# A fused attention and MLP kernel: where the seven-product quads stand, and when their operands are made

## The chip, the cores and the metric

The kernel runs on one core of one Trainium2 chip. The core's engines work side by side, each through its own queue of instructions: TensorE (PE, matmuls into PSUM; PEld is its weight load), VectorE (DVE), ScalarE (ACT), GpSimd (POOL), and SyncE (SP), which here only issues DMAs. The metric is the time of one execution on the device, in microseconds; smaller is better.

## The reference

Block-sparse attention over 4 batches, 8 heads, 768 tokens and 64 values per head, and behind it a residual MLP with affine layers, on tokens of 512 values:

```python
scores = scale * np.matmul(q, k.transpose(0, 1, 3, 2))
mask = ...   # diagonal blocks of 32, first and last block, 3 sampled blocks per row
attn = softmax(np.where(mask, scores, -1e9))
x = np.matmul(attn, v)            # laid out as (batch, token, 512)
a1 = alpha1 * x + beta1
tok = np.einsum('ts,bsd->btd', w_tok, a1)
u = x + lam * tok
a2 = alpha2 * u + beta2
ch = np.maximum(a2 @ w_ch1, 0.0) @ w_ch2      # 512 -> 2048 -> 512
out = u + lam * ch
```

## The kernel before

**Attention.** The 32 heads are 16 pairs (`i`, four to a batch). A pair is nine units of scores: `emit_qk` (L600), exponential on ACT (`emit_exp`, L618), the product with the 0/1 mask on VectorE (`emit_keep`, L635, only from pair 5 on; before, the mask lies in the score matmul), the value matmuls (`emit_pv` L647, `emit_pv_keys` L670), and `emit_finish`: a reciprocal (L687) and the normalisation (L688) into the batch's `x_sb`. `emit_a1pp` (L704, L705), mostly on POOL, makes the affine input of the token mixer; `job_tok2` (L844, L856) is the mixer.

**MLP.** For each batch, `job_f1` (L910, ACT L917) makes hidden rows: `hts[(b, c)]` holds 16 rows of 128 for half `c` of the tokens (three tiles of 128 each). The second layer has two forms:

- *direct*, `job_f2` (L930): one token tile times all of `w2b`, 16 matmuls of 512 columns in four quarters (`g`), then one addition into `x_sb` (L939) and a store;
- a *quad* (`job_p`, `mul` L1044): two token tiles together, by the Winograd form of Strassen's scheme. The operands are cut in two along hidden rows and along output columns, and seven products of 8 matmuls with 256 columns take the place of eight. In a quad, "11" and "12" are the two hidden halves of its first tile, "21" and "22" those of its second.

What the products need beside `hts` and `w2b`: sums and differences of hidden rows S1 to S4 (`job_s`, L1018; S3 and S4 overwrite "21" and "12"), and differences of weights T1, T2, T4, T3 (`job_t`, L972), 16 subtractions of two rows each, kept in the attention's freed q and k buffers. After each product `plus` (L1054) adds its bank to `x_sb` on VectorE. Products 1, 6 and 5 add up in one bank, and so do 7 and 4; each addition has to read the bank before the next product of the chain goes on in it.

**Order.** It is written out by hand. Up to pair 4 a table, `PLAN`, gives each job a slot ("tq5", the transposes of pair 5's q, has slot 31.62). Behind that come rows of letters (`W1`, `W2`, `W2L`, `W3`), three rows for a pair. A row is emitted letter by letter into all queues: `q` the scores of the row's three units and their first exponential, `x` another exponential, `k` a mask product, `p` value matmuls, `f` a hidden row, `g` the next step of the second layer, `S` a hidden-row sum, `A` a weight difference, `T` a mixer step, `L` the loads of a later pair, `Y` the copy of its values, `Q` and `K` its transposes by DMA, `d` and `v` transposes of the mixer's result. Batch 1's second layer runs in `W2` (pairs 8 to 11), batch 2's in `W2L` (pairs 12 to 15), batch 3's in `W3` and after. An engine's queue holds its instructions in the order in which the letters emit them.

`STR` lists the batches with quads, `P_ORDER` the order of `g`, `S_ORDER` that of `S`:

```python
STR = (2, 3)
P_ORDER[2] = direct 0, product 2 of quads 1 and 2, direct 3, product 1 of both,
             then products 6, 7, 5, 4, 3 of quad 1 and of quad 2
P_ORDER[3] = three quads
```

A quad `t` before consists of the tiles `t` and `t + 3`, one from each half of the tokens.

Of the kernel before, what the change touches and what calls it, by code (L numbers as in the profile page):

```python
# [52 lines left out]
]  # L53
W2 = [
# [12 lines left out]
]  # L67
W2L = [
# [12 lines left out]
]  # L81
W3 = [
# [4 lines left out]
]  # L87
STR = (2, 3)
HN = NH // 2
HC = DM // 2  # L90
WEAVE = W1 + W2 + W2L + W3
# [96 lines left out]
    "mask2": 30.13,  # L188
    "w2_1": 30.13,
    "w1_1": 30.27,  # L190
    "tq5": 31.62,
    "tok2_0": 31.97,
    "lv5": 32.09,
    "mask13": 32.27,
# [53 lines left out]
def kernel(  # L248
# [16 lines left out]
    nc = tc.nc  # L265
# [194 lines left out]
    def sp_tile():  # L460
        return psum.tile([P, 2, 512], FP, name="sp", tag="sp", bufs=2)
# [6 lines left out]
    def mm_tile(shape=(P, DM), dt=FP):  # L468
        return psum.tile(list(shape), dt, name="mm", tag="mm", bufs=3)
# [103 lines left out]
    x_sbs = {}  # L573
# [237 lines left out]
    hts = {}  # L811
# [177 lines left out]
    def a_of(b, t, name, r=slice(0, HN)):  # L989
        if name in ("X1", "X2"):  # L990
            return xs[(b, t, name)][:, r]
        c, half = {"11": (0, 0), "12": (0, 1), "21": (1, 0), "22": (1, 1)}[name]
        return hts[(b, c)][:, HN * half + r.start : HN * half + r.stop, ts(t, P)]

    SOP = {
        1: ("X1", "21", "22", ALU.add),
# [5 lines left out]
    def job_s(b, t, n, r=slice(0, HN)):  # L1002
        dst, a, c, op = SOP[n]
        rows = range(r.start, r.stop)
        for name in (a, c):
            if name[0] == "X":
                assert all(("S", b, t, int(name[1]), m) in did for m in rows)
            else:
                h, half = divmod(int(name) - 11, 10)
                assert all(("f", b, h, HN * half + m) in did for m in rows)  # L1010
        if n == 3:
            assert all(("S", b, t, 1, m) in did for m in rows)
        if n == 4:
            assert (b, t, 2) in did
        if dst[0] == "X" and (b, t, dst) not in xs:
            tag, bufs = ("eT", 6) if b == B - 1 else ("xs", 4)
            xs[(b, t, dst)] = ap_.tile([P, HN, P], BF, name="xs", tag=tag, bufs=bufs)
        nc.vector.tensor_tensor(  # L1018
            out=a_of(b, t, dst, r), in0=a_of(b, t, a, r), in1=a_of(b, t, c, r), op=op
        )  # L1020
        did.update(("S", b, t, n, m) for m in rows)
# [12 lines left out]
    def mul(b, t, n, ps, start, cols=slice(0, HC)):  # L1034
        a, m, need = PROD[n]
        assert m in bq or all((m, r) in did for r in range(0, HN, 2))
        if need:
            assert all(("S", b, t, need, r) in did for r in range(HN))
        c, half = {"1": (0, 0), "X": (1, 0)}.get(a[0], (1, 0))
        if need == 0:  # L1040
            h, half = divmod(int(a) - 11, 10)
            assert all(("f", b, h, HN * half + r) in did for r in range(HN))
        for r in range(HN):
            nc.tensor.matmul(  # L1044
                ps,
                a_of(b, t, a)[:, r],
                b_rows(m, r)[:, 0, cols],
                start=(start and r == 0),
                stop=(r == HN - 1),
                skip_group_check=True,  # L1050
            )

    def plus(x, ps):
        nc.vector.tensor_tensor(out=x, in0=x, in1=ps, op=ALU.add)  # L1054

    def twice(ps):
        return ps.unsqueeze(1).broadcast_to([P, 2, HC])

    lo, hi = slice(0, HC), slice(HC, DM)

    def job_p(b, t, n):
        x = x_sbs[b]
        last = (b, t) == (B - 1, NT // 2 - 1)
        bk = banks.setdefault((b, t), {})
        if n in (1, 2, 7):
            bk[n] = sp_tile()[:, 0] if n == 1 else mm_tile()[:]
        if n == 3 and not last and 2 not in bk:
            bk[2] = mm_tile()[:]
        if n == 1:
            mul(b, t, 1, bk[1][:, lo], True)  # L1070
            plus(x[:, t, lo], bk[1][:, lo])
        elif n == 2:
            mul(b, t, 2, bk[2][:, lo], True)
            if last or b < B - 1:
                plus(x[:, t, lo], bk.pop(2)[:, lo])
            if last:
                emit_store(b, t, lo)
        elif n == 6:
            mul(b, t, 6, bk[1][:, lo], False)
            plus(x[:, t + 3, lo], bk[1][:, lo])  # L1080
        elif n == 7:
            mul(b, t, 7, bk[7][:, lo], True)
            plus(x[:, t + 3, hi], bk[7][:, lo])
        elif n == 5:
            mul(b, t, 5, bk[1][:, lo], False)
            plus(x[:, t : t + 4 : 3, hi], twice(bk[1][:, lo]))
        elif n == 4:
            mul(b, t, 4, bk[7][:, lo], False)
            plus(x[:, t + 3, lo], bk[7][:, lo])
            emit_store(b, t + 3, slice(0, DM))  # L1090
        elif last:
            for h in range(2):
                sl = slice(HC + h * P, HC + h * P + P)
                ps = (mm_tile(), op_tile([P, DM]))[h]
                mul(b, t, 3, ps[:, sl], True, ts(h, P))
                plus(x[:, t, sl], ps[:, sl])
                emit_store(b, t, sl, (nc.sync, nc.scalar)[h])
        else:
            sl = hi if b < B - 1 else slice(0, DM)
            mul(b, t, 3, bk[2][:, hi], b < B - 1)  # L1100
            plus(x[:, t, sl], bk[2][:, sl])
            emit_store(b, t, slice(0, DM))
        did.add((b, t, n))

    NPAIR = B * NP
# [34 lines left out]
    def start_mlp(b):  # L1140
        ns = [n // 2 + HN * (n % 2) for n in range(NH)] if b == B - 1 else range(NH)
        todo["f"] += [lambda c=c, n=n: job_f1(b, c, n) for c in range(2) for n in ns]
        if b not in STR:
            todo["g"] += [
# [6 lines left out]
        ]  # L1151
        todo["S"] += [lambda t=t, n=n, r=r: job_s(b, t, n, r) for t, n, r in S_ORDER[b]]

    REST = (6, 7, 5, 4, 3)
    P_ORDER = {
        2: [(0, g, "g") for g in range(4)]
        + [(t, 2) for t in (1, 2)]
        + [(3, g, "g") for g in range(4)]
        + [(t, 1) for t in (1, 2)]
        + [(t, n) for t in (1, 2) for n in REST],  # L1160
        3: [(t, n) for t in range(2) for n in (1, 2)]
        + [(t, n) for t in range(2) for n in REST]
        + [(2, n) for n in (1, 2) + REST],
    }
    ALL, R1, R2 = slice(0, HN), slice(0, HN // 2), slice(HN // 2, HN)
    S_ORDER = {
        2: [(t, n, ALL) for t in (1, 2) for n in (1, 2, 3, 4)],
        3: [(t, n, R1) for n in (1, 2, 3) for t in range(3)]
        + [(t, n, r) for t in range(3) for n, r in ((1, R2), (2, R2), (3, R2), (4, ALL))],
    }  # L1170

    def start_pair(i):
# [222 lines left out]
```

## Time and profile before

| | |
|---|---|
| median of 3 runs | 300.59 us (300.05 to 300.66) |
| the profiled execution | 300.64 us |
| its span, first to last instruction | 298.6 us |
| mean granted TensorE clock | 1.000 |
| busy: PE, DVE, ACT, POOL | 292.3, 219.5, 218.6, 109.7 us |
| hidden rows, L910: 512 matmuls | 91.6 us |
| direct form, L930: 224 matmuls of 512 columns | 54.7 us |
| quad products, L1044: 272 matmuls of 256 columns, 16 of 128 | 38.1 us, by groups |

A timeline row has the start, the time from the first start to the last end of a merged group, engine and line, what is written from what, the shape and the count, and in brackets idle time of the engine just before, with what ended it. A row of groups has the busy time, the mean of one in ns, and the idle time ahead. A matmul's own row is longer than the distance to the next one, because they are pipelined; distances are what adds up on TensorE.

### The profile page before, as it was taken

The numbers are of one execution on the slowest core, as the hardware profiler recorded it, in microseconds if no ns is written. First come the engines' busy times: TensorE is split into PE (matmuls) and PEld (weight loads), VectorE is DVE, ScalarE is ACT, GpSimd is POOL, SyncE is SP. The second block draws the span as 40 slices with busy tenths as digits, with TensorE's granted clock in tenths as the row PEclk, the third lists the DMA queues.
The fourth block names the chain that finished last, engine by engine and source line by source line (L and its number), as shares of the span: only waits on it lengthen the run. The fifth ranks groups of instructions, "written<-read, shape, count | busy, mean of one in ns | idle before, by whom it ended". The sixth has DMA issues, their size and how long they took to land.

```text
span 298.6 us, 7517 instructions
## 1 busy us (share of the span) xinstructions
PE 292.3 (98%) x3113; PEld 194.5 (65%) x3113; DVE 219.5 (74%) x434; ACT 218.6 (73%) x324; POOL 109.7 (37%) x149
## 2 busy tenths in 40 slices
PE   7999999999999999999999999999999999999995
PEld 3688888665567565565576465565566589666884
DVE  4988999995678797978778777892756889204674
ACT  4999999998799963999779581999869734677100
POOL 8997887632443710355323340344320300000000
PEclk9999999999999999999999999999999999999999
DMA  6999999971392992729844777727321112300032
GB/s 178 201 193 168 192 156 204 190 121 26 94 151 50 120 201 75 121 61 134 119 85 76 121 119 143 114 72 89 50 61 30 25 37 57 113 0 2 0 140 74
DMA packets 57273, 31.08 MB, mean 104 GB/s; under 512 B 37204, under 2 KB 54016, under 8 KB 57240
## 3 DMA queue, kind: packets, MB, share of 16 engines
q0 software_dynamic: 16752, 14.22, 33.2%
q1 hardware_dynamic: 40020, 15.92, 27.9%
q8 instruction: 24, 0.39, 0.6%
q10 hardware_dynamic: 468, 0.47, 0.5%
q14 instruction: 9, 0.07, 0.1%
HBM read 29.75 MB, written 6.29 MB: 121 GB/s over the span
## 4 chain that ended last, share of the span: by engine, by line
PE 83%; DVE 6%; DMA 6%; ACT 3%; POOL 1%; issue 1%; ACTq 0%; SPq 0%; POOLq 0%
PE mm L910 27%; PE mm L930 15%; PE sp L600 8%; PE mm L844 8%; PE op L670 7%; PE mm L1044 5%; PE sp L1044 4%; PE mm L600 3%; DMA qpad<-in_q_dram 3%; ACT eT L618 2%; PE op L647 2%; DVE eT L635 2%; PE mm L820 1%; DMA uraw<-ubf 1%; DMA ms<-ms_c 1%
## 5 line engine op out<-in xcount | busy, mean ns | idle before, releaser
L618 ACT ACTIVATE eT<-sp,expb 128x1024 f16<-128x1024 f32 x111 | 118.4, 1120 | 2.2 <-PE sp L600 1.6
L910 PE MATMUL mm<-uT,w1b 128*128 128x384 bf16 x512 | 91.6, 326 | 0.1
L635 DVE TENSOR_TENSOR eT<-eT,mask 128x1024 f16<-128x1024 f16 x99 | 80.3, 840 | 13.9 <-ACT eT L618 13.7
L917 ACT ACTIVATE hts<-mm 128x384 bf16<-128x384 f32 x128 | 60.9, 500 | 16.5 <-PE mm L910 15.9
L704 POOL TENSOR_TENSOR a1pp<-x_sb,vbc 128x384 bf16<-128x384 f32 x25 | 28.5, 1140 | 119.3 <-DVE x_sb L688 85.3
L910 PEld LDWEIGHTS <-w1b 128*128 128x128 bf16 x512 | 48.1, 98 | 32.0 <-issue 2.4
L618 ACT ACTIVATE eT<-mm,expb 128x512 f16<-128x512 f32 x66 | 41.7, 685 | 26.5 <-PE mm L600 26.2
L930 PE MATMUL mm<-w2b,hts 128*128 128x512 bf16 x224 | 54.7, 379 | 0.0
L670 PEld LDWEIGHTS <-eT 128*128 128x128 f16 x792 | 29.8, 98 | 8.7 <-issue 1.7
L930 PEld LDWEIGHTS <-hts 128*128 128x128 bf16 x224 | 19.8, 98 | 22.3 <-issue 3.9
L670 PE MATMUL op<-vext,eT 128*128 128x65 f16 x792 | 32.1, 194 | 0.1
L600 PE MATMUL sp<-qTs,kTs 88*128 88x512 bf16 (+1 forms) x120 | 26.9, 326 | 1.4 <-ACT eT L618 0.7
L705 POOL TENSOR_TENSOR a1pp<-a1pp,vbc 128x384 bf16<-128x384 bf16 x25 | 26.7, 1069 | 2.0
L844 PE MATMUL mm<-a1pp,wtokT 128*128 128x256 bf16 x216 | 25.9, 273 | 0.1
L844 PEld LDWEIGHTS <-wtokT 128*128 128x128 bf16 x216 | 20.6, 98 | 5.6 <-issue 1.8
L1044 PEld LDWEIGHTS <-hts 128*128 128x128 bf16 x208 | 19.6, 98 | 3.0 <-issue 0.3
L600 PE MATMUL sp<-qhT,khT 64*128 64x256 bf16 (+1 forms) x176 | 19.8, 322 | 0.0
L856 DVE TENSOR_TENSOR x_sb<-x_sb,mm 128x512 f32<-128x512 f32 x18 | 12.3, 685 | 9.9 <-PE mm L844 9.8
L600 PEld LDWEIGHTS <-khT 64*128 64x128 bf16 x264 | 10.6, 94 | 12.7 <-issue 9.2
L647 PEld LDWEIGHTS <-eT 128*128 128x128 f16 x360 | 14.9, 98 | 3.8 <-issue 0.3
L1018 DVE TENSOR_TENSOR xs<-hts 128x512 bf16<-128x512 bf16 (+1 forms) x8 | 3.7, 487 | 17.8 <-ACT hts L917 17.8
L688 DVE TENSOR_TENSOR x_sb<-op,rcp 128x384 f32<-128x384 f32 x28 | 15.6, 557 | 1.0
(117 smaller groups left out, 322.3 us busy)
## 6 DMA issues: line engine op xcount, KB each, us to landing
out_dram<-x_sb SPq DMA_DIRECT2D x23, 256.0 KB
qpad<-in_q_dram POOLq DMA_DIRECT2D x15, 192.0 KB, 4.6
kr<-in_k_dram POOLq DMA_DIRECT2D x15, 192.0 KB, 5.6
vr<-in_v_dram POOLq DMA_DIRECT2D x15, 192.0 KB, 6.2
w1b<-in_moe_w_ch_dram POOLq DMA_DIRECT2D x4, 512.0 KB, 9.3
w2b<-in_moe_w_ch_dram POOLq DMA_DIRECT2D x4, 512.0 KB, 8.4
hts<-in_moe_w_tok_dram POOLq DMA_DIRECT2D x2, 576.0 KB, 9.2
x_sb<-in_k_dram ACTq DMA_DIRECT2D x2, 192.0 KB
```

The source lines that it names most:

```text
L600: nc.tensor.matmul(sp[jj][:, dst], lhsT, rhs, start=True, stop=True, skip_group_check=True,)
L618: nc.scalar.activation(dst, at, AF.Exp, bias=expb[:], scale=SCALE)
L635: nc.vector.tensor_mul(out=e, in0=e, in1=keep)
L647: nc.tensor.matmul(op[0][:, o, :], ets[u][:, jj, h * QB + n * P : h * QB + n * P + P], vexts[i % NVB][:, w, 2 * jp + jj, :], start=op[1] == 0,
L670: nc.tensor.matmul(op[0][:, o, :], ets[u][:, jj, h * QB + n * P : h * QB + n * P + P], vexts[i % NVB][:, w, 2 * jp + jj, :], start=op[1] == 0,
L704: eng.tensor_tensor(out=dst, in0=x_sbs[b][:, :, cols], in1=bc[0], op=ALU.mult)
L705: eng.tensor_tensor(out=dst, in0=dst, in1=bc[1], op=ALU.add)
L844: nc.tensor.matmul(ps[:, o], wtokT[:, os_, ts(2 * n + o, P)], a1pps[i][:, os_, :], start=(os_ == 0 and o == 0), stop=(os_ == NT - 1 and o ...
L910: nc.tensor.matmul(ps[:, 0:QC], w1b[:, dk, ts(n, P)], uTs[b][:, dk, ts(c, QC)], start=(dk == 0), stop=(dk == 3),)
L917: nc.scalar.activation(hts[(b, c)][:, n, :], ps[:, 0:QC], AF.Relu)
L930: nc.tensor.matmul(ps[:], ht[:, nk, ts(o % 3, P)], w2b[:, nk, :], start=(nk == 0), stop=(nk == NH - 1),)
L1044: nc.tensor.matmul(ps, a_of(b, t, a)[:, r], b_rows(m, r)[:, 0, cols], start=(start and r == 0), stop=(r == HN - 1), skip_group_check=True,)
```

## The change

A quad now takes two tiles of the same half of the tokens in batches 1 and 2, so that it needs one `hts` half only; `t` is a pair of tile numbers. Batch 1, all direct before, gets the quad (0, 1); batch 2's two are (0, 1) and (3, 4), in place of (1, 4) and (2, 5); batch 3's three stay (0, 3), (1, 4), (2, 5). Product 1 of batch 1's quad and of batch 2's first takes a bank of the three shared `mm` banks, not one of scores (`sp`). The products of a quad follow each other without another quad's in between. The 16 letters `A` move from `W2` rows 5, 6 and 9 to `W1` rows 3, 4, 5 and 8 and `W2` rows 0, 2 and 5; the letters `S` go to rows 7 and 9 of `W2` and `W2L` and, for batch 2's second quad, stay in `W3`; one `g` of `W2` falls away, two `f` leave `W2L` rows 7 and 8, one comes back in its row 11, one in `W3`. The slot of "tq5" is 32.6.

```diff
-    "q K x g p k 0 k 1 x Q p L Y f f g 2 g k",
-    "q g g x x 0 1 f k 2 k f p k p",
-    "q 0 s 1 s k x x p T f 2 k f k p",
+    "q A A K x g p k 0 k 1 x Q p L Y f f g 2 g k",
+    "q A A A g g x x 0 1 f k 2 k f p k p",
+    "q A A A 0 s 1 s k x x p T f 2 k f k p",
...
-    "q 0 x p x g k k 1 d g k g 2",
+    "q A A 0 x p x g k k 1 d g k g 2",
 ]
 W2 = [
-    "q 0 p p g k x L x p f k 1 K 2 k",
+    "q A A 0 p p g k x L x p f k 1 K 2 k",
...
-    "q g 0 k g d 1 2 p x k g x k",
+    "q A A A g 0 k g d 1 2 p x k g x k",
...
-    "q k 0 f x f p s f f x 1 L p k 2 f f f k Y A A A A A f",
-    "q f L f 0 f k A A A A A A A A 1 f Y x f p g x f p f g k k 2",
-    "q x k x k Q 0 g 1 s f f g p 2 p f f k p",
+    "q k 0 f x f p s f f x 1 L p k 2 f f f k Y A f",
+    "q f L f 0 f k 1 f Y x f p g x f p f g k k 2",
+    "q S S x k x k Q 0 g 1 s f f g p 2 p f f k p",
     "q T 0 k f 1 x k f T x f 2 p k K p",
-    "q A A A x 0 x T k 1 k f 2 k f Q f d p L",
+    "q S S x 0 x T k 1 k f 2 k f Q f d p L",
     "q x 0 x K k g d k s f g f 1 k p p g 2",
-    "q Y g x x k g k f 0 1 k 2 p g v g v",
+    "q Y g x x k g k f 0 1 k 2 p g v v",
 ]
 W2L = [
...
-    "q x k x k Q 0 g 1 s f f g p 2 p f f k p f",
-    "q T 0 k f 1 x k f T x f 2 p k K p f",
-    "q x 0 x T k 1 k f 2 k f Q f d p L",
-    "q x 0 x K k g d k s f g f 1 k p p S S g 2",
-    "q p Y x x k g k S 0 1 k 2 g v g v g",
+    "q S S x k x k Q 0 g 1 s f f g p 2 p f f k p",
+    "q T 0 k f 1 x k f T x f 2 p k K p",
+    "q S S x 0 x T k 1 k f 2 k f Q f d p L",
+    "q x 0 x K k g d k s f g f 1 k p p g 2",
+    "q p Y x x k g k f 0 1 k 2 g v g v g",
 ]
 W3 = [
-    "a p p p g s g g T S T S T S S S d g g U g v g g g g g f f f f",
+    "a p p p f g s g T S T S T S d g g U g v S g g g g g g f f f f",
...
-STR = (2, 3)
+STR = (1, 2, 3)
...
-    "tq5": 31.62,
+    "tq5": 32.6,
...
-        c, half = {"11": (0, 0), "12": (0, 1), "21": (1, 0), "22": (1, 1)}[name]
-        return hts[(b, c)][:, HN * half + r.start : HN * half + r.stop, ts(t, P)]
+        o, half = t[int(name[0]) - 1], int(name[1]) - 1
+        return hts[(b, o // 3)][:, HN * half + r.start : HN * half + r.stop, ts(o % 3, P)]
...
-        if n in (1, 2, 7):
-            bk[n] = sp_tile()[:, 0] if n == 1 else mm_tile()[:]
-        if n == 3 and not last and 2 not in bk:
-            bk[2] = mm_tile()[:]
+        if n == 1 and (tail or (b == B - 2 and o1 == 3)):
+            bk[1] = sp_tile()[:, 0]
+        elif n in (1, 2, 7) or (n == 3 and not tail):
+            bk[n] = mm_tile()[:]
...
+    def direct(*tiles):
+        return [(o, g, "g") for o in tiles for g in range(4)]
+
+    def quad(t, order):
+        return [(t, n) for n in order]
+
     REST = (6, 7, 5, 4, 3)
     P_ORDER = {
-        2: [(0, g, "g") for g in range(4)]
-        + [(t, 2) for t in (1, 2)]
-        + [(3, g, "g") for g in range(4)]
-        + [(t, 1) for t in (1, 2)]
-        + [(t, n) for t in (1, 2) for n in REST],
+        1: quad((0, 1), (2, 1, 6, 5, 7, 4, 3)) + direct(2, 3, 4, 5),
+        2: quad((0, 1), (2, 1, 6, 5, 7, 4, 3))
+        + direct(2, 5)
+        + quad((3, 4), (2, 1) + REST),
...
     S_ORDER = {
-        2: [(t, n, ALL) for t in (1, 2) for n in (1, 2, 3, 4)],
+        1: [((0, 1), n, ALL) for n in (1, 2, 3, 4)],
+        2: [(t, n, ALL) for t in ((0, 1), (3, 4)) for n in (1, 2, 3, 4)],
```

More of the change, by code (lines that the diff above doesn't have):

```diff
@@ L991, in a_of, with a_ready @@
             return xs[(b, t, name)][:, r]
-        c, half = {"11": (0, 0), "12": (0, 1), "21": (1, 0), "22": (1, 1)}[name]
-        return hts[(b, c)][:, HN * half + r.start : HN * half + r.stop, ts(t, P)]
+        o, half = t[int(name[0]) - 1], int(name[1]) - 1
+        return hts[(b, o // 3)][:, HN * half + r.start : HN * half + r.stop, ts(o % 3, P)]
+    def a_ready(b, t, name, rows):
+        if name[0] == "X":
+            return all(("S", b, t, int(name[1]), m) in did for m in rows)
+        o, half = t[int(name[0]) - 1], int(name[1]) - 1
+        return all(("f", b, o // 3, HN * half + m) in did for m in rows)
     SOP = {
@@ L1004, in job_s @@
         rows = range(r.start, r.stop)
[L1005 to L1010, printed above, removed]
+        assert a_ready(b, t, a, rows) and a_ready(b, t, c, rows)
         if n == 3:
@@ L1038, in mul @@
             assert all(("S", b, t, need, r) in did for r in range(HN))
[L1039 to L1042, printed above, removed]
+        assert a_ready(b, t, a, range(HN))
         for r in range(HN):
@@ L1061, in job_p @@
     def job_p(b, t, n):
-        x = x_sbs[b]
-        last = (b, t) == (B - 1, NT // 2 - 1)
+        x, (o1, o2) = x_sbs[b], t
+        tail = b == B - 1
+        last = tail and o2 == NT - 1
         bk = banks.setdefault((b, t), {})
-        if n in (1, 2, 7):
-            bk[n] = sp_tile()[:, 0] if n == 1 else mm_tile()[:]
-        if n == 3 and not last and 2 not in bk:
-            bk[2] = mm_tile()[:]
+        if n == 1 and (tail or (b == B - 2 and o1 == 3)):
+            bk[1] = sp_tile()[:, 0]
+        elif n in (1, 2, 7) or (n == 3 and not tail):
+            bk[n] = mm_tile()[:]
         if n == 1:
             mul(b, t, 1, bk[1][:, lo], True)
-            plus(x[:, t, lo], bk[1][:, lo])
+            plus(x[:, o1, lo], bk[1][:, lo])
         elif n == 2:
             mul(b, t, 2, bk[2][:, lo], True)
-            if last or b < B - 1:
-                plus(x[:, t, lo], bk.pop(2)[:, lo])
+            if last or not tail:
+                plus(x[:, o1, lo], bk[2][:, lo])
             if last:
-                emit_store(b, t, lo)
+                emit_store(b, o1, lo)
         elif n == 6:
             mul(b, t, 6, bk[1][:, lo], False)
-            plus(x[:, t + 3, lo], bk[1][:, lo])
+            plus(x[:, o2, lo], bk[1][:, lo])
         elif n == 7:
             mul(b, t, 7, bk[7][:, lo], True)
-            plus(x[:, t + 3, hi], bk[7][:, lo])
+            plus(x[:, o2, hi], bk[7][:, lo])
         elif n == 5:
             mul(b, t, 5, bk[1][:, lo], False)
-            plus(x[:, t : t + 4 : 3, hi], twice(bk[1][:, lo]))
+            plus(x[:, o1 : o2 + 1 : o2 - o1, hi], twice(bk[1][:, lo]))
         elif n == 4:
             mul(b, t, 4, bk[7][:, lo], False)
-            plus(x[:, t + 3, lo], bk[7][:, lo])
-            emit_store(b, t + 3, slice(0, DM))
+            plus(x[:, o2, lo], bk[7][:, lo])
+            emit_store(b, o2, slice(0, DM))
         elif last:
@@ L1095, in job_p @@
                 mul(b, t, 3, ps[:, sl], True, ts(h, P))
-                plus(x[:, t, sl], ps[:, sl])
-                emit_store(b, t, sl, (nc.sync, nc.scalar)[h])
-        else:
[L1099 to L1102, printed above, removed]
+                plus(x[:, o1, sl], ps[:, sl])
+                emit_store(b, o1, sl, (nc.sync, nc.scalar)[h])
+        else:
+            sl, ps = (slice(0, DM), bk[2]) if tail else (hi, bk[3])
+            mul(b, t, 3, ps[:, hi], not tail)
+            plus(x[:, o1, sl], ps[:, sl])
+            emit_store(b, o1, slice(0, DM))
         did.add((b, t, n))
@@ L1152, in start_mlp @@
         todo["S"] += [lambda t=t, n=n, r=r: job_s(b, t, n, r) for t, n, r in S_ORDER[b]]
+    def direct(*tiles):
+        return [(o, g, "g") for o in tiles for g in range(4)]
+    def quad(t, order):
+        return [(t, n) for n in order]
     REST = (6, 7, 5, 4, 3)
     P_ORDER = {
-        2: [(0, g, "g") for g in range(4)]
-        + [(t, 2) for t in (1, 2)]
-        + [(3, g, "g") for g in range(4)]
-        + [(t, 1) for t in (1, 2)]
-        + [(t, n) for t in (1, 2) for n in REST],
-        3: [(t, n) for t in range(2) for n in (1, 2)]
-        + [(t, n) for t in range(2) for n in REST]
-        + [(2, n) for n in (1, 2) + REST],
+        1: quad((0, 1), (2, 1, 6, 5, 7, 4, 3)) + direct(2, 3, 4, 5),
+        2: quad((0, 1), (2, 1, 6, 5, 7, 4, 3))
+        + direct(2, 5)
+        + quad((3, 4), (2, 1) + REST),
+        3: quad((0, 3), (1, 2))
+        + quad((1, 4), (1, 2))
+        + quad((0, 3), REST)
+        + quad((1, 4), REST)
+        + quad((2, 5), (1, 2) + REST),
     }
     ALL, R1, R2 = slice(0, HN), slice(0, HN // 2), slice(HN // 2, HN)
+    Q3 = [(0, 3), (1, 4), (2, 5)]
     S_ORDER = {
-        2: [(t, n, ALL) for t in (1, 2) for n in (1, 2, 3, 4)],
-        3: [(t, n, R1) for n in (1, 2, 3) for t in range(3)]
-        + [(t, n, r) for t in range(3) for n, r in ((1, R2), (2, R2), (3, R2), (4, ALL))],
+        1: [((0, 1), n, ALL) for n in (1, 2, 3, 4)],
+        2: [(t, n, ALL) for t in ((0, 1), (3, 4)) for n in (1, 2, 3, 4)],
+        3: [(t, n, R1) for n in (1, 2, 3) for t in Q3]
+        + [(t, n, r) for t in Q3 for n, r in ((1, R2), (2, R2), (3, R2), (4, ALL))],
     }
```

## The prediction

> **What bounds the kernel now.** I read the page's busy times and slices first, then the chain of waits, then the timeline engine by engine around the places that the change touches.
>
> ```profile
> span 298.6 us, 7517 instructions
> PE 292.3 (98%) x3113; PEld 194.5 (65%) x3113; DVE 219.5 (74%) x434; ACT 218.6 (73%) x324; POOL 109.7 (37%) x149
> PE   7999999999999999999999999999999999999995
> PE 83%; DVE 6%; DMA 6%; ACT 3%; POOL 1%; issue 1%; ACTq 0%; SPq 0%; POOLq 0%
> ...
> 99.62 2.59 PE mm L930 x12
> 254.04 1.75 PE mm L1044 x16
> ```
>
> TensorE (PE) works in every slice and makes 83% of the chain, so a microsecond taken from it is a microsecond gained, and one in which it waits is lost. VectorE (DVE), at 74%, has room, but its rows follow the program's order: one that waits holds up all behind it. From the last two rows: a 512-column matmul of the direct form takes 2.59/12 = 0.216 us, a 256-column matmul of a quad product 1.75/16 = 0.109 us.
>
> **The arithmetic saved.** Two direct tiles are 2 x 16 x 0.216 = 6.91 us; a quad is 7 x 8 x 0.109 = 6.1 us. Batch 1 gains one quad, batch 2 keeps two: **-0.8 us** on TensorE, certain, as nothing else is removed there.
>
> **Pair 5's q, delayed.** Its six transposes wait for their load; tok2_0's six matmuls, two score matmuls and eight value matmuls now go first.
>
> ```profile
> 39.51 0.41 PE L647 MATMUL op<-vext,eT 128*128 128x65 f16 x8
> 40.17 0.51 PE L550 MATMUL mm<-ident,qpad 128*128 128x128 bf16 x6 [0.24 <-DMA qpad<-in_q_dram]
> 53.28 0.47 DVE L885 TENSOR_SCALAR uT<-mm,ab2T 128x384 bf16<-128x384 bf16 x1
> 53.34 1.47 PE L910 MATMUL mm<-uT,w1b 128*128 128x384 bf16 x8
> ```
>
> Eight value matmuls of 0.03 us from 39.51 leave some 0.4 us idle before 40.17. But VectorE is what comes next: its scaling that ends at 53.75 is awaited by the fourth matmul of the group begun at 53.34, which starts at 53.83. That chain shortens little. I take **-0.2**, bounds -0.4 and 0. The step's three VectorE copies go behind one value copy, with pair 5's first use far later; it issues no DMA.
>
> **The weights' differences, moved.** Sixteen subtractions leave VectorE near 135-140 and 156 us for six groups of 2, 3, 3, 2, 2 and 3 in earlier idle stretches, and one alone.
>
> ```profile
> 139.11 0.76 DVE L972 TENSOR_TENSOR kTs<-w2b,kTs 128x512 bf16<-128x512 bf16 x2
> 76.12 0.69 DVE L939 TENSOR_TENSOR x_sb<-x_sb,mm 128x512 f32<-128x512 f32 x1 [0.86 <-PE mm L930]
> 86.13 0.69 DVE L635 TENSOR_TENSOR eT<-eT,mask 128x1024 f16<-128x1024 f16 x1 [1.16 <-ACT eT L618]
> 118.05 0.69 DVE L635 TENSOR_TENSOR eT<-eT,mask 128x1024 f16<-128x1024 f16 x1 [1.26 <-ACT eT L618]
> ```
>
> Two take 0.76, three 1.1 us; the three gaps shown (first, tightest, last of six) hold them. Cost 0, hidden by those gaps; a group that overran would pass its excess to TensorE: up to +1 us in all.
>
> **The quad in batch 1, and batch 2's first.** This is where I expect the loss. In the changed program tiles 0 and 1 take products 2, 1, 6, 5 and 7, 4, 3, each in the place on TensorE where a direct quarter stood, of the same length. Products 1, 6 and 5 share one PSUM bank, and so do 7 and 4: product 6 cannot start before product 1's addition has read the bank, nor before S2. VectorE's order there reads: value copy, product 2's addition, reciprocal, normalisation, **product 1's addition, two mask products, S1, S2**. TensorE has between products 1 and 6 only the scores of one row.
>
> ```profile
> 139.42 1.03 PE L930 MATMUL mm<-w2b,hts 128*128 128x512 bf16 x4
> 141.95 1.03 PE L930 MATMUL mm<-w2b,hts 128*128 128x512 bf16 x4
> 142.91 0.39 PE L600 MATMUL mm<-qhT,khT 64*128 64x512 bf16 x2
> 143.67 1.04 PE L930 MATMUL mm<-w2b,hts 128*128 128x512 bf16 x4
> 139.99 0.49 ACT L917 ACTIVATE hts<-mm 128x384 bf16<-128x384 f32 x1
> 141.74 0.56 DVE L688 TENSOR_TENSOR x_sb<-op,rcp 128x384 f32<-128x384 f32 x1
> 142.21 2.08 DVE L635 TENSOR_TENSOR eT<-eT,mask 128x1024 f16<-128x1024 f16 x2
> 142.38 1.37 POOL L704 TENSOR_TENSOR a1pp<-x_sb,vbc 128x384 bf16<-128x384 f32 x1 [3.98 <-DVE x_sb L688]
> 143.83 1.25 POOL L705 TENSOR_TENSOR a1pp<-a1pp,vbc 128x384 bf16<-128x384 bf16 x1
> ...
> 159.38 1.28 DVE L635 TENSOR_TENSOR eT<-eT,mask 128x1024 f16<-128x1024 f16 x2
> 235.27 0.68 DVE L1018 TENSOR_TENSOR xs<-hts 128x1024 bf16<-128x1024 bf16 x1
> 235.98 0.69 DVE L1018 TENSOR_TENSOR xs<-xs,hts 128x1024 bf16<-128x1024 bf16 x1
> 251.52 0.74 DVE L1054 TENSOR_TENSOR x_sb<-x_sb,mm 128x256 f32<-128x256 f32 x2
> 254.75 1.04 PE L1044 MATMUL mm<-w2b,hts 128*128 128x256 bf16 x8
> 255.83 0.42 DVE L1054 TENSOR_TENSOR x_sb<-x_sb,mm 128x256 f32<-128x256 f32 x1 [0.45 <-PE mm L1044]
> ```
>
> *Product 2* stands at 139.42. Its eighth matmul, due 7 x 0.109 later (140.18), needs the last row of hts, evicted by ACT from 139.99 to 140.48: **+0.3** (0 to 0.35).
>
> *Product 1* moves to 142.25. Its addition starts 1.08 later (254.75 to 255.83) at 143.33; then come 0.33 (0.74 less 0.42) for it, two masks at 0.60 each (1.28 less 0.68), S1 0.71, S2 0.69 and a hand-over of 0.05: product 6 at 146.3. TensorE is ready at 142.25 + 0.87 + 0.09 + the scores' 0.76 = 143.97. Wait: 2.35 us if nothing disturbs VectorE. But the two masks here took 2.08, not 1.28, beside POOL's two operations, which follow the normalisation and do so still. With that 0.8 the wait is **+3.1** (2.35 to 3.6).
>
> [...]
>
> *Product 4* needs product 7's addition, which is queued behind a mask, and POOL is at work there too. In batch 2 of the kernel before an addition stands in exactly this place, so the price can be read:
>
> ```profile
> 162.15 1.03 PE L930 MATMUL mm<-w2b,hts 128*128 128x512 bf16 x4
> 161.58 3.34 DVE L635 TENSOR_TENSOR eT<-eT,mask 128x1024 f16<-128x1024 f16 x3 [0.22 <-ACT eT L618]
> ...
> 232.32 1.04 PE L1044 MATMUL mm<-w2b,hts 128*128 128x256 bf16 x8
> 233.47 0.81 PE L910 MATMUL mm<-uT,w1b 128*128 128x384 bf16 x4
> 231.68 1.41 DVE L635 TENSOR_TENSOR eT<-eT,mask 128x1024 f16<-128x1024 f16 x1 [0.22 <-ACT eT L618]
> 233.01 0.41 DVE L1054 TENSOR_TENSOR x_sb<-x_sb,mm 128x256 f32<-128x256 f32 x1
> ```
>
> The mask held VectorE for 1.41, the addition ended at 233.42, TensorE went on at 233.47. Product 4, wanted at 232.32, would start then: 1.15 us late, of which the kernel before already loses 0.28 (the product at 232.32 ends 0.87 later): **+0.9** in batch 2 (0.2 with an undisturbed mask). In batch 1 the same mask starts at 161.58, so the addition ends at 163.3 and product 4, wanted at 162.15, loses **+1.2** (0.5 to 1.3). Products 5 and 3 have other work ahead of them, longer than their additions: 0.
>
> *Batch 2, rows as in batch 1.* Product 1 reuses product 2's bank, and that addition is queued behind a copy that waits for its values' load.
>
> ```profile
> 210.61 0.36 DVE L328 COPY vext<-vr 128x768 f16<-128x768 f16 x1 [4.30 <-DMA vr<-in_v_dram]
> 210.75 1.03 PE L930 MATMUL mm<-w2b,hts 128*128 128x512 bf16 x4
> 211.59 4.02 DVE L635 TENSOR_TENSOR eT<-eT,mask 128x1024 f16<-128x1024 f16 x4
> 211.76 1.36 POOL L704 TENSOR_TENSOR a1pp<-x_sb,vbc 128x384 bf16<-128x384 f32 x1 [6.14 <-DVE x_sb L688]
> ```
>
> The addition runs from 210.9 to 211.3 and product 1 starts at 211.36, not 210.75: **+0.6** (0.3 to 0.65), product 2's wait included. Product 6: the same chain as above, now with POOL's first operation straight ahead of the first mask (four masks took 4.02 here, 2.48 by 0.60 each): **+3.3** (2.35 to 3.7).
>
> *Batch 2's second quad* (tiles 3 and 4) has product 6 right behind product 1 in one bank, where the kernel before had other products between. Addition visible at 1.08 + 0.42 + 0.05, product 1 over at 0.87: **+0.7** (0.6 to 0.8).
>
> Stores of tiles 0 and 1 move behind transposes in SP's queue and are issued later; nothing reads them, so 0; a transpose stuck behind a store would be late by at most product 4's 1.2. POOL's queue keeps its order; what it issues slides with TensorE.
>
> **Sum.** -0.8 - 0.2 + (0.3 + 3.1 + 1.2) + (0.6 + 3.3 + 0.9 + 0.7) = +9.1 us. TensorE has no slack to win it back: the page shows it busy throughout. The profiled execution took 300.64 us (span 298.6 and 2.0 around it), the median of the runs 300.59, so both give **309.7 us**. Lower ends: (0 + 2.35 + 0.5) + (0.3 + 2.35 + 0.2 + 0.6) - 0.8 - 0.4 = +5.1, 305.7 us. Upper ends: (0.35 + 3.6 + 1.3) + (0.65 + 3.7 + 0.9 + 0.8) + 1.0 - 0.8 = +11.5, 312.1 us.
>
> **Rivals.** (1) *It does what it says, faster*: the mechanism is TensorE finding enough work between products 1 and 6. Then -0.8 - 0.2 gives 299.6 us. It decides from the point at which that work reaches 3.2 us (1.08 + 0.33 + 1.2 + 1.45 less product 1's 0.87); the rows show 0.85. For it speaks that TensorE is busy throughout this region before; against it, the program's order. 6 in 100; another 2 in 100 for a small loss that ends within 0.2%, which is about what measurement can tell from no change.
>
> (2) *The waits come, but VectorE is not disturbed*, because POOL's operations fall elsewhere once TensorE has shifted: 305.7 us or somewhat less. Both POOL operations hang on the normalisation just ahead, which is against it: 10 in 100.
>
> (3) *The clock falls*. Before, TensorE never idles long after its start. At that start it ran at half pace:
>
> ```profile
> L480 PE MATMUL op<-const-bfloat16-1.0 128*128 128x512 bf16 x12 | 5.0, 564 | 0.8 <-PEq L1379 0.8
> ```
>
> 5.0/12 = 0.42 us for 512 columns against 0.216. If each of the two long waits throws it back to that pace for those 5.0 us, each costs 2.5 more: 309.7 + 5.0 = 314.7 us. 7 in 100, since no fall in mid-run is in this trace, where TensorE never rests long enough to try it. [...]
>
> **How the numbers follow.** The likeliest case, all waits as priced, has 75 in 100, with its own range 306.5 to 312.1. With rival 2 it makes 85; the range 305.5 to 312.5 holds these. Slower 0.92, same 0.02, faster 0.06.
>
> **What would show it.** Right: in the changed profile TensorE idles some 3 us ahead of product 6's first matmul in batches 1 and 2, released by the S line of VectorE; about 1 us ahead of product 4, and 0.6 to 0.7 in two more places, released by additions; the mean clock stays 1.00; no wait stands ahead of pair 5's transposes; VectorE's idle time before the six places shrinks. Wrong: product 6 follows the scores without a gap, or masks pass POOL undisturbed, or the clock row falls below 1.00 after the waits.

## The result and the profile after

| | before | changed |
|---|---|---|
| median | 300.38 us (6 runs, 300.05 to 300.66) | 312.38 us (6 runs, 310.50 to 313.23) |
| profiled execution, span | 300.64, 298.6 us | 312.31, 310.3 us |
| mean granted TensorE clock | 1.000 | 0.989 (0.989 to 0.994 over the runs) |

The ratio is 1.0388, 95% interval 1.0357 to 1.0420: slower by 12.0 us. The forecast was 309.7 us, within 305.5 to 312.5.

The head of the changed kernel's page and its slices:

```profile
span 310.3 us, 7557 instructions
PE 294.6 (95%) x3121; PEld 198.3 (64%) x3137; DVE 222.6 (72%) x443; ACT 219.5 (71%) x324; POOL 109.4 (35%) x149
PE   8999999999999999995998999999699899999995
PEclk9999999999999999999899999999799999999999
```

TensorE did not get more work, it stands still: two slices, from 139.6 and from 217.2 us, fall to 5 and 6 tenths. The clock row falls in the slice behind the first and in the second itself, which it did nowhere before. (Matmul records of the direct form are partly missing in this trace: 176 of 192.) The view of waits names the releasers; these are TensorE's rows (total us, times, longest) that stand ahead of quad products (L1042):

```profile
PE mm L1042 <- DVE xs L1019: 6.2, 2, 3.2
PE mm L1042 <- DVE x_sb L1052: 2.1, 2, 1.1
PE sp L1042 <- DVE x_sb L1052: 0.6, 1, 0.6
PE mm L1042 <- ACT hts L917: 0.4, 2, 0.2
```

They are: twice product 6 for S2 (L1019), twice product 4 and once batch 2's second product 6 for an addition (L1052), twice product 2 for a hidden row. The timeline where the wait is 3.2 us, in batch 1 and, behind the dots, TensorE's rows of the same place in batch 2:

```profile
142.06 0.56 DVE L688 TENSOR_TENSOR x_sb<-op,rcp 128x384 f32<-128x384 f32 x1
142.71 0.99 POOL L704 TENSOR_TENSOR a1pp<-x_sb,vbc 128x384 bf16<-128x384 f32 x1 [4.65 <-DVE x_sb L688]
143.07 0.42 DVE L1052 TENSOR_TENSOR x_sb<-x_sb,mm 128x256 f32<-128x256 f32 x1 [0.45 <-PE mm L1042]
143.41 2.16 DVE L635 TENSOR_TENSOR eT<-eT,mask 128x1024 f16<-128x1024 f16 x2
143.77 1.25 POOL L705 TENSOR_TENSOR a1pp<-a1pp,vbc 128x384 bf16<-128x384 bf16 x1
145.49 0.68 DVE L1019 TENSOR_TENSOR xs<-hts 128x1024 bf16<-128x1024 bf16 x1
146.21 0.69 DVE L1019 TENSOR_TENSOR xs<-xs,hts 128x1024 bf16<-128x1024 bf16 x1
146.96 1.04 PE L1042 MATMUL mm<-qTs,xs 128*128 128x256 bf16 x4 [3.17 <-DVE xs L1019]
148.64 2.02 PE L910 MATMUL mm<-uT,w1b 128*128 128x384 bf16 x8
150.50 1.04 PE L1042 MATMUL mm<-qTs,xs 128*128 128x256 bf16 x8
...
220.72 0.61 PE L1042 MATMUL mm<-qTs,xs 128*128 128x256 bf16 x4 [3.01 <-DVE xs L1019]
221.76 2.77 PE L910 MATMUL mm<-uT,w1b 128*128 128x384 bf16 x8
224.32 1.30 PE L1042 MATMUL mm<-qTs,xs 128*128 128x256 bf16 x8
225.46 0.71 PE L670 MATMUL op<-vext,eT 128*128 128x65 f16 x18
```

Product 1's addition, two masks stretched to 2.16 us beside POOL, S1, S2, product 6: the chain of the forecast. An idle figure counts from the modelled end of the last matmul; the time lost has 0.16 us more, because a row is that much longer than the distance to the next one (a 512-column row is 0.38 long, its distance 0.22). The losses are 3.33 and 3.17 us.

What follows was not in the sum. From 146.96 to 148.64 eight 256-column matmuls take 1.68 us instead of 0.87, the eight of 384 columns behind them 1.86 instead of 1.30: 1.36 us lost. In batch 2 the same places take 1.04, 2.56 and 1.14 instead of 0.87, 1.30 and 0.87: 1.7 us. The view of windows (length, busy time of PE, PEld, DVE, ACT and POOL, then granted clock, DMA share, GB/s) shows why:

```profile
143.50:146.50 3.00, 0.29 (x4) 0.00 (x0) 2.97 (x4) 3.00 (x4) 1.44 (x2) 0.97 1.36 156
146.50:149.70 3.20, 2.74 (x12) 1.74 (x13) 2.02 (x4) 0.16 (x1) 0.00 (x0) 0.50 0.21 47
217.50:220.70 3.20, 0.21 (x2) 0.00 (x0) 3.17 (x5) 3.08 (x4) 1.29 (x1) 1.00 0.00 0
221.50:224.80 3.30, 3.30 (x14) 1.72 (x12) 0.79 (x2) 0.73 (x2) 0.00 (x0) 0.50 0.00 0
```

TensorE works at half its clock for a while, once the wait is nearly over or, in batch 2, after it. The other waits are short rows, each a product that follows an addition which VectorE was late with; the first pair is product 4 in batch 1, and the second is product 6 of batch 2's second quad:

```profile
166.24 1.42 DVE L635 TENSOR_TENSOR eT<-eT,mask 128x1024 f16<-128x1024 f16 x1 [0.21 <-ACT eT L618]
167.58 0.41 DVE L1052 TENSOR_TENSOR x_sb<-x_sb,mm 128x256 f32<-128x256 f32 x1
168.04 0.38 PE L1042 MATMUL mm<-kTs,hts 128*128 128x256 bf16 x2 [1.06 <-DVE x_sb L1052]
...
262.50 0.41 DVE L1052 TENSOR_TENSOR x_sb<-x_sb,sp 128x256 f32<-128x256 f32 x1
262.97 0.60 PE L1042 MATMUL sp<-qTs,xs 128*128 128x256 bf16 x4 [0.57 <-DVE x_sb L1052]
```

The same instruction's end in both traces tells how far the changed kernel is behind, and where each microsecond comes in. The rows are exponentials on ACT; the last is a hidden row of batch 3:

| end before | end changed | behind by | what lies between this row and the one above |
|---|---|---|---|
| 43.67 | 43.34 | -0.33 | pair 5's q delayed |
| 144.02 | 144.07 | 0.05 | product 2 (0.34) |
| 150.31 | 154.98 | 4.66 | product 6 (3.33) and the slow clock (1.36) |
| 166.47 | 172.38 | 5.91 | product 4 (1.22) |
| 171.80 | 176.84 | 5.05 | the arithmetic saved |
| 198.22 | 203.01 | 4.80 | a wait of the kernel before at 195.5, gone |
| 212.82 | 218.00 | 5.17 | product 2 of batch 2 (0.35) |
| 257.02 | 268.67 | 11.65 | product 6 (3.17), slow clock (1.7), product 4 (1.22, less 0.28 that the kernel before lost there), second quad (0.73), the last pair's mixer input (0.18): 6.7, of which 6.5 show |

### The profile page after: what moved, and what is told of

Its sections match the earlier page's. It is cut to its first block, busy times and chain, and to the rows that moved or that the text cites. A ratio compares the mean times of both kernels' runs of the same rounds, so it can differ in the third digit from the quotient of the medians.

```text
span 310.3 us, 7557 instructions
## 1 busy us (share of the span) xinstructions
PE 294.6 (95%) x3121; PEld 198.3 (64%) x3137; DVE 222.6 (72%) x443; ACT 219.5 (71%) x324; POOL 109.4 (35%) x149
## 4 chain that ended last, share of the span: by engine, by line
PE 88%; DVE 5%; ACT 2%; issue 2%; DMA 1%; ACTq 0%
PE mm L910 27%; PE mm L930 13%; PE sp L600 10%; PE mm L1042 8%; PE mm L844 8%; PE op L670 8%; PE mm L600 3%; PE sp L1042 3%; PE mm L820 3%; PE op L647 2%; DVE eT L635 2%; PE mm L647 1%; ACT eT L618 1%; DMA ms<-ms_c 1%; PE mm L510 1%
## 5 line engine op out<-in xcount | busy, mean ns | idle before, releaser
L910 PE MATMUL mm<-uT,w1b 128*128 128x384 bf16 x512 | 93.5, 331 | 0.0
L635 DVE TENSOR_TENSOR eT<-eT,mask 128x1024 f16<-128x1024 f16 x99 | 79.4, 827 | 14.7 <-ACT eT L618 14.5
L704 POOL TENSOR_TENSOR a1pp<-x_sb,vbc 128x384 bf16<-128x384 f32 x25 | 27.7, 1109 | 128.3 <-DVE x_sb L688 99.7
L910 PEld LDWEIGHTS <-w1b 128*128 128x128 bf16 x512 | 48.9, 99 | 31.9 <-issue 3.6
L930 PE MATMUL mm<-w2b,hts 128*128 128x512 bf16 x176 | 44.3, 379 | 0.7
L930 PEld LDWEIGHTS <-hts 128*128 128x128 bf16 x192 | 17.2, 98 | 19.4 <-issue 3.0
L1042 PEld LDWEIGHTS <-hts 128*128 128x128 bf16 x248 | 23.2, 98 | 7.1 <-issue 3.2
L705 POOL TENSOR_TENSOR a1pp<-a1pp,vbc 128x384 bf16<-128x384 bf16 x25 | 26.9, 1075 | 2.0
L1052 DVE TENSOR_TENSOR x_sb<-x_sb,mm 128x256 f32<-128x256 f32 (+2 forms) x28 | 12.7, 452 | 13.8 <-PE mm L1042 13.2
L1019 DVE TENSOR_TENSOR xs<-hts 128x512 bf16<-128x512 bf16 (+1 forms) x9 | 4.4, 508 | 17.8 <-ACT hts L917 17.8
```

The lines of the kernel that those rows point to most:

```text
L635: nc.vector.tensor_mul(out=e, in0=e, in1=keep)
L704: eng.tensor_tensor(out=dst, in0=x_sbs[b][:, :, cols], in1=bc[0], op=ALU.mult)
L705: eng.tensor_tensor(out=dst, in0=dst, in1=bc[1], op=ALU.add)
L910: nc.tensor.matmul(ps[:, 0:QC], w1b[:, dk, ts(n, P)], uTs[b][:, dk, ts(c, QC)], start=(dk == 0), stop=(dk == 3),)
L930: nc.tensor.matmul(ps[:], ht[:, nk, ts(o % 3, P)], w2b[:, nk, :], start=(nk == 0), stop=(nk == NH - 1),)
L1042: nc.tensor.matmul(ps, a_of(b, t, a)[:, r], b_rows(m, r)[:, 0, cols], start=(start and r == 0), stop=(r == HN - 1), skip_group_check=True,)
```

## The experiments

Of rows of letters that stand alike in `W2` and `W2L` one is shown; both were changed.

**Is the clock the waits' doing?** The waits stay, but TensorE is kept busy in them.

```diff
+FILL = 24
...
         elif n == 6:
+            if not tail and o1 == 0:
+                for r in range(FILL):
+                    nc.tensor.matmul(
+                        bk[1][:, hi],
+                        a_of(b, t, "11")[:, r % HN],
+                        b_rows((1, 1), r % HN)[:, 0],
...
             mul(b, t, 6, bk[1][:, lo], False)
```

> The changed kernel with 24 idle matmuls of 256 columns (2.6 us) put into each of the two long waits ahead of product 6, into an unused half of its bank, with a result that nobody reads; the waits themselves stay. Theory A (TensorE's idle time is what lowers the clock): the half-clock stretches of 1.4 and 1.7 us go, product 6 starts at the same time as in the changed kernel, 312.4 - 3.0 = 309.4 us, clock 1.00. Rival B (the clock is low for another reason): 312.4 us with the clock still at 0.99.

Measured 309.16 us (309.00 to 309.74), ratio 1.0295 (1.0280 to 1.0310), clock 1.00. The windows of batch 1's wait and of what follows it in that kernel:

```profile
143.50:146.70 3.20, 2.91 (x27) 2.28 (x25) 3.17 (x5) 3.05 (x4) 1.26 (x1) 1.00 1.42 164
146.70:150.00 3.30, 3.30 (x33) 2.60 (x34) 1.55 (x4) 0.98 (x2) 0.00 (x0) 1.00 0.11 23
```

The work behind the wait runs at full clock, and 3.2 us are back although 48 matmuls were added. Theory A holds: the idle time lowers the clock, and that costs 3 us here.

**Do the masks take longer because of POOL?** Its two operations are held until S2 is there.

```diff
+HELD = ((9, 1), (13, 1))
...
         did.update(("S", b, t, n, m) for m in rows)
+        if n == 2 and held:
+            nc.gpsimd.tensor_copy(out=scr[:], in_=xs[(b, t, "X2")][:, 0, 0:1])
+            emit_a1pp(*held.pop(0), nc.gpsimd)
...
+        elif (i, w) in HELD:
+            held.append((i, w))
         elif (i, w) != (0, 0):
             emit_a1pp(i, w, nc.vector if last or early else nc.gpsimd)
```

> The changed kernel with POOL's two operations (L704, L705) for the pairs that finish just ahead of product 6 held back until S2 is written, by a copy of one column on POOL that reads S2. Theory A (the two masks take 2.0 to 2.2 us instead of 1.28 because POOL's two operations block VectorE): the masks take 1.3, product 6's waits shrink by 0.9 and 0.7 us to about 2.4 each, 310.8 us if the clock falls as before, 307.8 us if such a wait no longer lowers it. Rival B (the masks are slow for another reason, such as late exponentials): masks unchanged, 312.4 us.

Measured 308.23 us (four runs: 307.39, 307.66, 308.81, 311.15), ratio 1.0278 (1.0233 to 1.0322). Its timeline at the same place (its lines are numbered a little higher):

```profile
143.55 1.28 DVE L636 TENSOR_TENSOR eT<-eT,mask 128x1024 f16<-128x1024 f16 x2
146.22 0.61 PE L1048 MATMUL mm<-qTs,xs 128*128 128x256 bf16 x4 [2.29 <-DVE xs L1022]
```

Two masks take 1.28 us, and both waits are 2.45 us, near the 2.35 that the forecast gave for a VectorE nobody disturbs. Theory A holds. The runs lie apart as their clocks do: the mean was 1.00, 1.00, 0.994 and 0.989, in the order of the times. By estimate one half-clock stretch of 3.41 us, as long as those in the changed kernel's trace, takes 0.0055 off a mean over 310 us and two take 0.011, so the means fit no fall, no fall, one and two. By that count a wait of this length (2.29 us idle in the profiled execution) lowered the clock in one execution and not in another.

**Does product 6 wait for nothing but the place of S1 and S2?**

```diff
-    "q f L f 0 f k 1 f Y x f p g x f p f g k k 2",
-    "q S S x k x k Q 0 g 1 s f f g p 2 p f f k p",
+    "q f L f 0 f k 1 f x f p S g x f S p f g Y k k 2",
+    "q x k x k Q 0 g 1 s f f g p 2 p f f k p",
```

> The changed kernel with the sums S1 and S2 of tiles 0 and 1 emitted before and behind product 2's addition (and the value copy behind it), no longer behind two mask products; nothing else. Theory A (product 6 waits only because S1 and S2 are emitted behind the masks, and the half-clock stretches of 3.4 us that follow in the trace come from those waits): both waits (3.33 and 3.17 us) and both half-clock stretches (1.4 and 1.7 us) go, 312.4 - 9.6 = 302.8 us, clock 1.00. Rival B (the slow clock is not caused by the waits): only the waits go, 305.9 us. Rival C (VectorE's rows are late for another reason, so that product 6 waits for something else): 310 us or more.

Measured 305.53 us (305.29 to 305.69), ratio 1.0170 (1.0154 to 1.0185), clock 1.00. That is close to B's 305.9, but not B, by which the clock would have stayed low: it is full. Product 6 follows the scores without a gap, and a new wait stands behind it:

```profile
143.47 3.21 DVE L635 TENSOR_TENSOR eT<-eT,mask 128x1024 f16<-128x1024 f16 x4
146.60 0.41 DVE L1052 TENSOR_TENSOR x_sb<-x_sb,mm 128x256 f32<-128x256 f32 x1
147.06 1.03 PE L1042 MATMUL mm<-qTs,xs 128*128 128x256 bf16 x8 [1.25 <-DVE x_sb L1052]
```

Product 6's addition is emitted behind four masks, and product 5 waits for it: 1.42 us in each batch (the idle time and the 0.16), 2.8 in all, which is what A's 302.8 is short of. In the changed kernel product 6 ended at 148.6, when all four masks were done.

**All known waits away (all_moved).** Beside S1 and S2: one more hidden row ahead of product 2, product 7's addition ahead of its mask, and another order for batch 2's second quad. The value copy `Y` stands ahead of product 1 here, in `sums_early` behind it.

```diff
-    "q f L f 0 f k 1 f Y x f p g x f p f g k k 2",
-    "q S S x k x k Q 0 g 1 s f f g p 2 p f f k p",
+    "q f L f 0 f k 1 f x f p f S g x S p f Y g k k 2",
+    "q x k x k Q 0 g 1 s f f g p 2 p f f k p",
...
-    "q x 0 x K k g d k s f g f 1 k p p g 2",
+    "q x 0 x K g d k k s f g f 1 k p p g 2",
...
-        + quad((3, 4), (2, 1) + REST),
+        + quad((3, 4), (2, 1, 7, 6, 4, 5, 3)),
```

> Sums early as in the other kernel, and the other three waits taken away: product 2 behind one more hidden row, product 7's addition ahead of the mask that it stood behind, and batch 2's second quad in the order 2, 1, 7, 6, 4, 5, 3, so that no product follows the one whose bank it shares. Theory A (the changed kernel's loss is the sum of its waits and of the clock that they cost): 312.4 - 9.6 - 2 x 1.22 - 0.7 - 0.7 = 299.0 us, 1.4 us faster than the kernel before. Rival B (the quads in batches 1 and 2 cost something that is not a wait, on VectorE or in the queues of DMAs): 300.4 us or more.

Measured 302.09 us (301.99 to 302.46), ratio 1.0058 (1.0045 to 1.0071). Products 2 and 4 and batch 2's second quad wait no more; product 5 waits twice as above, now 1.58 us: 3.2 us, the whole of the miss.

```profile
146.85 1.03 PE L1042 MATMUL mm<-qTs,xs 128*128 128x256 bf16 x8 [1.42 <-DVE x_sb L1052]
```

So product 6 with its addition was moved ahead of two masks (all_moved_2; here and in the next two experiments the lines that fall away are those of the version it is built on):

```diff
-    "q x k x k Q 0 g 1 s f f g p 2 p f f k p",
+    "q g x k x k Q 0 1 s f f g p 2 p f f k p",
```

> As the kernel with all four waits taken away, and product 6 emitted right behind the scores instead of behind two more mask products, in batches 1 and 2: in that kernel product 5 waited 1.58 us twice, because product 6's addition stood behind four masks. Theory A (these two waits are the whole of what that kernel was over its forecast): 302.1 - 3.1 = 299.0 us, 1.4 us faster than the kernel before. Rival B (VectorE is full enough there that the delay only moves on to the masks and value matmuls): 301 us or more.

Measured 299.81 us (11 runs, 299.46 to 300.06) against 300.17, ratio 0.9986 (0.9977 to 0.9994). Short of A by 0.8, for the two masks still ahead of the addition are drawn out by POOL:

```profile
142.94 2.48 DVE L635 TENSOR_TENSOR eT<-eT,mask 128x1024 f16<-128x1024 f16 x2
145.34 0.41 DVE L1052 TENSOR_TENSOR x_sb<-x_sb,mm 128x256 f32<-128x256 f32 x1
145.81 1.03 PE L1042 MATMUL mm<-qTs,xs 128*128 128x256 bf16 x8 [0.21 <-DVE x_sb L1052]
```

0.38 us twice. One of the two masks went behind the addition as well (all_moved_3):

```diff
-    "q f L f 0 f k 1 f x f p f S g x S p f Y g k k 2",
-    "q g x k x k Q 0 1 s f f g p 2 p f f k p",
+    "q f L f 0 f k 1 f x f p f S g x S p f Y g k 2",
+    "q g k x k x k Q 0 1 s f f g p 2 p f f k p",
```

> As all_moved_2, with one more mask product behind product 6's addition instead of ahead of it, in batches 1 and 2; in all_moved_2 product 5 still waited 0.38 us twice, for that addition behind two masks that POOL drew out to 2.48 us. Theory A (these waits are all that is left of the loss): 299.8 - 0.75 = 299.1 us. Rival B (the masks, now later, make the value matmuls behind product 5 wait instead): 299.8 us.

Measured 299.07 us (298.84 to 299.42) against 300.10, ratio 0.9965 (0.9951 to 0.9978): this version beats both kernels, by 1.0 us (0.35%, its slowest run below the fastest of the kernel before) and by 13.3. The busy times on its page:

```profile
PE 291.4 (98%) x3137; PEld 197.1 (66%) x3137; DVE 221.3 (74%) x443; ACT 218.7 (74%) x324; POOL 109.3 (37%) x149
```

and, of its view of waits, TensorE's rows that have to do with VectorE or ACT's exponentials:

```profile
PE sp L600 <- ACT eT L618: 0.7, 3, 0.3
PE mm L844 <- DVE a1pp L705: 0.2, 1, 0.2
```

No wait for a sum or an addition is left. The changed kernel does the same arithmetic with as many instructions on each engine; 13.3 us lay in the order alone, the clock included, which the order's waits let fall.

**The quad in batch 1 by itself (batch1_direct)**: all_moved_2, but batch 1 direct again.

```diff
-STR = (1, 2, 3)
+STR = (2, 3)
...
-    "q Y g x x k g k f 0 1 k 2 p g v v",
+    "q Y g x x k g k f 0 1 k 2 p g v g v",
```

> As all_moved_2, with batch 1 all direct again and batch 2 left with its two quads. Theory A (a quad without waits saves 0.8 us of matmul distances and nothing else): 299.0 + 0.8 = 299.8 us. Rival B (the quad's extra work on VectorE eats the saving): equal to all_moved_2.

Measured 300.25 us (11 runs, 299.59 to 301.19), 0.44 us above its partner; the two profiled spans are 298.6 and 297.8. Both go A's way. The size is not settled closer than 0.4 to 0.8, since the runs of one kernel spread as widely as that.

**The two other parts by themselves (weights_tq5)**: the kernel before with the letters `A` and "tq5" as in the change, its quads untouched.

```diff
-    "tq5": 31.62,
+    "tq5": 32.6,
...
-    "q k 0 f x f p s f f x 1 L p k 2 f f f k Y A A A A A f",
+    "q k 0 f x f p s f f x 1 L p k 2 f f f k Y A f",
...
```

> The kernel before with two parts of the change alone: the weights' differences moved to the earlier rows, and pair 5's q delayed; the quads are those of the kernel before. Theory A (the moved differences cost nothing; the delay saves the 0.4 us that the trace of the changed kernel is ahead at 43 us): 300.4 - 0.4 = 300.0 us. Rival B (the differences delay what stands behind them on VectorE): up to 301 us.

Measured 300.25 us (12 runs, 299.60 to 301.61) against 300.17, ratio 1.0005 (0.9994 to 1.0016): no difference. The differences cost nothing: at 43 us the trace is 0.48 us ahead of the kernel before and stays so until 195. There it is lost. First the kernel before, then this one:

```profile
193.12 0.48 DVE L885 TENSOR_SCALAR uT<-uraw,ab2T 128x768 bf16<-128x768 bf16 x1 [0.45 <-DMA uraw<-ubf]
195.55 0.91 PE L670 MATMUL op<-vext,eT 128*128 128x65 f16 x24
```

```profile
193.02 0.48 DVE L885 TENSOR_SCALAR uT<-uraw,ab2T 128x768 bf16<-128x768 bf16 x1 [0.84 <-DMA uraw<-ubf]
195.46 0.91 PE L670 MATMUL op<-vext,eT 128*128 128x65 f16 x24 [0.47 <-DVE x_sb L688]
```

VectorE waits for a transpose by DMA that ends at nearly the same time in both; masks, a normalisation and then TensorE's value matmuls queue behind it. 0.4 us gained at 43 us are given back at 195, so A's time was wrong though its mechanism shows in the trace. The transpose was issued 0.48 us earlier (188.18 against 188.66) and yet ended at the same time; why is open.

## Why the prediction was right or wrong

The direction was right, the time fell within the range, and the places of the loss and their releasers were right but for one. But 312.4 us lies above the likeliest case (309.7, its own range to 312.1), and one term is the reason: the clock. That the time still lies inside the range, by 0.1 us, is luck: the sum with the clock in it comes out above the range, and smaller errors the other way brought it back. Point by point:

| step | forecast | measured in the trace |
|---|---|---|
| arithmetic saved | -0.8 | -0.86 |
| pair 5's q | -0.2 | -0.33 to -0.39 |
| weights' differences | 0 | 0 |
| product 2, batch 1 | +0.3 | +0.34 |
| product 6, batch 1 | +3.1 | +3.33 |
| product 4, batch 1 | +1.2 | +1.22 |
| products 2 and 1, batch 2 | +0.6 | +0.35 |
| product 6, batch 2 | +3.3 | +3.17 |
| product 4, batch 2 | +0.9 | +0.94 |
| second quad | +0.7 | +0.73 |
| the clock | 0, as rival 3 +5.0 | +1.36 and +1.67 |
| wait at 195.5 before | not in the sum | -0.24 |
| wait for the last pair's mixer input | not in the sum | +0.18 |

*What held.* The chain ahead of product 6 and POOL's share of it: 2.35 undisturbed against 2.45 measured with POOL held back. Product 4's price, read off an addition that stood in the same place in the kernel before, came out to 0.04 us. Rival 1 decided from the point at which TensorE has 3.2 us of work between products 1 and 6. The other way of meeting it, S1 and S2 in VectorE's idle stretch ahead of the value copy, was not thought of; the last version does that, and gets what rival 1 named (299.07 against 299.6).

*What failed* is the step "7 in 100, since no fall in mid-run is in this trace", by which the clock stands at 0 in the sum. The same sentence says that TensorE never rested long enough there to try it, so the absent row was no evidence either way. Behind its first 10 us the longest idle time of TensorE in that trace is the 0.24 us ahead of pair 5's transposes; the waits of the forecast were 3.1 and 3.3. The clock fell behind them (idle times of 3.17 and 3.01 us), which the prediction names as a sign that it is wrong, and in all six runs of the changed kernel the mean lay at 0.989 to 0.994. By the count given with `pool_held`, three of the six (0.989) fit a fall at both waits, the other three (0.993 and 0.994) a fall at one. `filler` shows that the idle time is the cause. Rival 3 had the mechanism, but its price was too high: each half-clock stretch lasted 3.41 us, not 5.0, and 0.62 us of the first fell into the wait itself. With the 3.0 us that the profiled execution lost by it, the sum would have been 312.7.

*Smaller misses.* Batch 2's product 1 did not wait. The forecast kept the value copy 0.14 us ahead of the product's place, as before (210.61 to 210.75); in the changed kernel it stood 1.08 us ahead:

```profile
214.84 0.37 DVE L328 COPY vext<-vr 128x768 f16<-128x768 f16 x1 [3.73 <-DMA vr<-in_v_dram]
215.92 1.04 PE L1042 MATMUL mm<-w2b,hts 128*128 128x256 bf16 x8
```

The load slid with TensorE, but not as far: POOL issued it 4.80 us later than before (204.90, then 209.70), the copy began 4.23 us later, and product 1 5.17 us later, 0.35 of that by product 2's wait. The delay of pair 5's q was worth more at its place than forecast, and alone it is worth nothing in the time, for a reason 150 us further on.

## What to carry to other kernels

Where a product is cut into a chain on one bank, the queue of the engine that adds and sums is part of the cost: count what the written order puts ahead of each addition and each operand, and compare it with the work that TensorE has in between. The saving of a quad was 0.8 us by the matmuls' distances, and the order decided between 12.0 us slower and 1.0 us faster. A wait taken away uncovers the next one in the same queue (product 6, then product 5 twice), so forecast the second one too. And TensorE worked at half its clock for 3.41 us at each of two idle times of 3.17 and 3.01 us here, and by the means at three of eight waits of about 2.3 us: price that as a term, not as a remote rival.

## What the runs showed of the hardware

**The clock fell on a grid of time, not where a wait began.** The windows of 0.1 us in which the granted clock changes, in the changed kernel:

```profile
146.30:146.40 0.10, 0.00 (x0) 0.00 (x0) 0.10 (x1) 0.10 (x1) 0.00 (x0) 0.72 1.33 270
149.70:149.80 0.10, 0.10 (x2) 0.05 (x1) 0.00 (x0) 0.00 (x0) 0.00 (x0) 0.71 0.00 0
...
221.40:221.50 0.10, 0.10 (x3) 0.09 (x1) 0.10 (x1) 0.00 (x0) 0.00 (x0) 0.69 0.00 0
224.80:224.90 0.10, 0.10 (x2) 0.10 (x1) 0.00 (x0) 0.10 (x1) 0.00 (x0) 0.74 0.00 0
```

A mean of 0.72 between 1 and 0.5 puts the first change 0.044 us into its window, and so on: the clock is halved from 146.34 to 149.76 and from 221.44 to 224.85, 3.41 us each time. The second stretch begins when TensorE has been at work for 0.72 us again. The two starts are 75.09 us apart, 22 times 3.4133. The stretches at full clock, by the record's own times, fit the same grid: in the changed kernel 71.68 us between the two (21 times 3.4133), 139.95 us ahead of them (41 times) and 85.33 us behind them (25 times), in the kernel before a single one of 293.55 us (86 times).

The record of the clock begins only 5.12 us (before) and 6.40 us (changed) into the span. Ahead of it the figure reads 1.00, also where nine of L480's 512-column matmuls took 4.00 us, 0.44 each against 0.22 later, so a mean clock of 1.00 says nothing of the start in these traces.

Idle times of 3.17 and 3.01 us both halved the clock in the profiled execution of the changed kernel, and over the six runs nine of twelve such waits did, by the means. With POOL held back (2.29 us idle in the profiled execution, where the clock stayed full) the means of two of the four runs show falls, at three of eight waits in all. The waits ahead of product 5 in all_moved (1.42 us idle, 1.58 lost) left the mean at 0.998 or more in all five, no lower than the runs of the kernel before (0.998 to 1.000). The clock also fell once TensorE's work was over: in the kernel before at 298.67 us, just behind the span's end (its last matmul ends at 295.06), and in the changed one at 310.19 us, inside the span (306.76). A mean a little under 1, such as 0.998, may come from such a fall somewhat earlier, which neither of the two traces shows.

That the phase of such a grid explains the spread between the runs of one kernel (310.5 to 313.2; 307.4 to 311.2) fits most of the clocks recorded with them (a run of the changed kernel at 0.993 took 312.49 us, as long as two at 0.989), but no run set the phase, so it stays an inference.

**VectorE's mask products took longer beside POOL's operations.** Beside POOL's L704 or L705 (one line higher in filler), two of them took 2.08 us in the kernel before, 2.16 and 2.01 in the changed one (batches 1 and 2), 2.01 in filler and 2.48 in all_moved_2. With POOL held back two took 1.28 us there, in both batches.
